# The second product of an MLP in seven quarter products, on groups of 256 tokens

## The chip, the cores and the metric

The kernel runs on one core of one Trainium2 chip. The metric is the device time in microseconds (us), the median of several runs. The profile of the kernel comes from one execution that the hardware profiler recorded.

## The reference, cut to what matters

An attention in blocks, then a layer that mixes by Fourier transforms, then an MLP with two products. There are 4 batches of 768 tokens; a token has 512 numbers (8 heads of 64).

```python
P = sort_net                                   # (4, 8, 8, 8), five rounds of normalizing
k_sorted = einsum('bhij,bhjcd->bhicd', P, k_b) # 8 blocks of 96 tokens, mixed by P
v_sorted = einsum('bhij,bhjcd->bhicd', P, v_b)
attn = softmax(0.125 * q_b @ k_sorted.T)       # inside each block
x = attn @ v_sorted                            # -> (4, 768, 512)
...
u  = x + real(fft(fft(x, axis=1), axis=2))
un = (u - mean(u)) / sqrt(var(u) + 1e-6)
out = u + maximum(un @ w_ch1, 0) @ w_ch2       # 512 -> 2048 -> 512
```

## The kernel before, in words

The work of a batch b falls into three parts.

The **attention**: q and k are loaded as fp16 and turned or mixed on PE (`q_mix`, L785; `k_mix`, L806), v is mixed (`v_mix`, L746) and moved to another layout by DMA (`v_move`, L768). Scores are made on PE (L838), reduced on DVE (L848, L883), raised to the exponential on ACT (L865, L877), and multiplied with the values (L922); DVE normalizes into the tile xr (L928, L929).

The **Fourier part**, which with the norm is called by `post` (L1344): sums and differences of xr on DVE (`fold`, L945, L950), a product over the tokens (`dft_s`, L968 to L990, result W, evacuated by ACT or DVE), sums over W (`fold_d`, L1005), a product over the 512 numbers (`dft_d`, L1030, result PQ by L1043). `residual` (L1073) brings x back to the token order of the output on PE, a copy makes u of it, and `add_res` adds PQ on POOL (L1085, L1086). Then follow the statistics (`stats`, L1100), `root` (L1109, L1113), the normalized un (`normal`, L1123 on ACT or L1126 on DVE), and its transposed form unT (`transpose_u`, L1138 by DMA; in batch 0 on PE, L1147). Tokens come in six tiles of 128, in pairs i = 0, 1, 2 with m = 0, 1.

The **MLP** (`mlp`, L1154) works on two groups of 384 tokens, three tiles, for each batch. For each of 16 chunks of the 2048 hidden numbers, four matmuls with 384 columns make a PSUM bank (L1165), and a relu on ACT or DVE takes it to the fp16 tile hr (L1171). Then, for each of the three tiles of tokens, 16 matmuls with 512 columns add up in a bank (L1183), in four steps of four; one instruction on DVE adds u / 64 and writes the tile outt (L1192), and `store` (L1197) sends it out: by POOL's indirect DMA (L1204), or, for the last two tiles of the last batch, in pieces on SP's and ACT's queues (L1200). All steps of the first and second product write the key "mlp", so that they stay in their written order among themselves.

Nothing of the order between the parts is written out by hand. Each piece of work is a *step* with the engines that can do it and a planned time on each; the planner (`Plan.run`, L396) takes again and again the step that can begin earliest by its own estimate and, among those within 43 ns, the one with the smallest `prio`. The MLP's products have a large prio, so they fill in where others wait; its relus and additions a very small one. The table LEAD (L222) shifts the prio of each kind of step in each batch, and REL (L219) is a time before which a load may not be issued. Loads of q, k, v and of the weights are issued by POOL, one after the other, and before some of them POOL waits, by a small copy (L478), until an earlier one has landed. Up to 69.5 us in the plan, products of the tile junk, which nobody reads, fill the gaps of PE (`fill`, L314; L672).

Buffers are *rings* of tiles: a step that opens a new buffer waits until one in the ring is free. Among them are hr (4 tiles of 4 x 384), u (10), outt (2), unT (2 of 4 x 384), k16 and q16 (3 each), v16 (6) and W (6). The rings k16x and q16x, for batch 0's last pair of heads, lie in a tile of unT. The PSUM has eight banks, one ring.

Of the kernel before, what the change touches and what calls it, by code (L numbers as in the profile page):

```python
# [9 lines left out]
F32 = mybir.dt.float32  # L10
# [5 lines left out]
B = 4  # L16
# [191 lines left out]
class Plan:  # L208
# [4 lines left out]
        psWe=271, psF=430, psR=324, psRh=162, psY=213, ph=640, pc=853, psG=640, psP=60, pcol=60)  # L213
# [8 lines left out]
    LEAD = dict(P=(-69.2, -25.6, 17, -26.9), Q=(0, 14.9, 40, -12.3), We=(2, 19, -0.7, 70.5),  # L222
        Wo=(0, 0, 0, 23.8), a16=(-11.2, 7.7, 69.1, 26.1), a_out=(-16.9, -30.9, -61.8, 4.9),
        add=(-68, 5.4, -30.8, 2.5), amr=(0.9, 0, 0, 0), amt=(-21.4, -19.4, 13.3, 0.1), const=(-1.3, 0, 0, 0),
        exp=(0, -0.4, -24.7, 32.2), fold=(0, -82.7, 0, 0), fold_d=(0, -2.5, -54.6, 0),
        kron=(7.9, 44.5, 27.4, -22.8), kz=(9, 8.3, 19.2, 0), load_k16=(0, 28.3, 2.3, -64.5),
        load_q16=(0, -5, -46.4, -2.3), load_v=(0, 0, 3.1, -3.3), m8=(80.4, 0, 0, 0),
        max=(-23.2, 0, -3.8, -60.5), minus=(50.2, -10.8, -54.2, 2.7), nm=(-36.9, 0, 3.8, 0),
        norm=(-18.9, -61.5, 39.2, 7.1), nse=(-0.9, 0, 0, 0), ot=(14.4, -11.7, -26.5, -37.8),
        outt=(-1.1, 0, 0, -20.8), patch=(77.1, 10.6, 45.9, 21.8), pc=(0, 0, -20.1, 11.7),  # L230
        pca=(-15.9, 0, 0, 0), pcol=(-26, 0, 0, 0), pcs=(-61.4, 0, 0, 0), ph=(-9.7, -14, -8.2, 0),
        psA=(0, -33.9, -24.3, 8.2), psB=(-0.4, 28.7, 8.4, 0), psF=(-46, 22.6, 30, 0), psG=(32.8, 0, 0, 0),
        psK=(6, 17.3, 37.2, 0.7), psM=(2.1, 0, 0, 0), psN=(-31.8, 6.5, 1.2, 0), psP=(-1.1, 0, 0, 0),
        psQ=(59.9, -3.6, 23.4, -2.4), psQK=(0, -29.6, -48.9, -3.2), psR=(12.8, -23.4, 14.8, 14.1),
        psRh=(22.2, 19.3, -2.1, 43.2), psS=(2.6, -28.9, 6.6, 7.3), psT=(14.6, -52.6, 0, 0),
        psV=(-1, 3.9, 20.1, 0), psWe=(38.7, 48, 12, -46.7), psWo=(-4.2, -52.6, -3.4, 8.4),
        psX=(-12.9, 43.1, 13.7, 0), psY=(36, 25.5, 0, 0), psaT=(-20.7, -10.8, 9.5, 1.7),
        ptm=(-45.9, 0, 0, 0), qT=(24.8, 10, 25, 71.4), relu=(0, 0, 0, -22.8), root=(-32.4, 55.6, 42.1, 9),
        row_zero=(-0.4, -51.2, -52.1, -17.7), stats=(10.4, 3.3, 0, 23.2), store=(-20.3, -23.1, -20.8, -3.4),
        turn_e=(0, 0, -27.5, 18.7), u=(-4.7, 56.1, 0, 0.9), un=(58.1, 22, 0, 40.1), unT=(44, 62.4, 0, 15.1),  # L240
        v_move=(0, 21.7, -15.7, 0), v_sum=(0, 0, 28.6, -13.1), vg=(4.3, 0, 0, 0), vo=(-77.8, 6.8, 0, 4.8),
        weights=(9.5, 0, 0, 0), xem=(-0.8, 85.8, -36.2, -9.1), xom=(-50.3, -12.2, 0.6, 0))
# [202 lines left out]
def kernel(  # L445
# [36 lines left out]
    def ring(tag, n, shape, dtype):  # L482
# [938 lines left out]
```

## Time and profile before

| what | value |
|---|---|
| median of 3 runs | 299.06 us (298.74 to 299.49) |
| the profiled execution, first to last instruction (its span) | 300.9 us |
| mean granted clock of PE | 0.979 |
| first product of the MLP (L1165) | 512 matmuls of 384 columns |
| second product (L1183) | 384 matmuls of 512 columns, from 93.6 us on |
| relu (L1171) | 128, 59.9 us on ACT |
| addition of u (L1192) | 24, 16.4 us on DVE |
| last addition begins | 295.68 us |

The profile gives the profiled execution's time as its span alone; it lies 1.8 us above the median of the runs. A line such as `L1165 PE MATMUL bank<-unT,w1sb ... x512 | 89.5, 326 | 1.4 <-DMA ...` names the line of the kernel, the engine, the operation, the tile written and those read, the shape, and the count; then the busy time in us and the mean of one in ns; then how long the engine idled just before such instructions and for what. PE is the matrix engine, PEld its weight loads, DVE the vector engine, ACT the one for functions, POOL and SP the two others. A matmul's duration holds its way through the array, so matmuls that follow each other closely overlap; their true rate is read from a run of them in the chain of waits. The slices cut the span into 40 parts of 7.5 us.

### The profile page before, as it was taken

How to read it: one execution, taken by the hardware profiler on the slowest of the kernel's cores; microseconds unless marked ns; L12 is line 12 of the kernel's file. 1: busy time of each engine (PE TensorE's matmuls, PEld its weight loads, DVE VectorE, ACT ScalarE, POOL GpSimd, SP SyncE). 2: the span in 40 equal slices, each digit the busy share in tenths (PEclk: the TensorE clock that was granted, in tenths of full speed). 3: DMA queues.
4: the chain of work that ended last, by engine and by line, in shares of the span. 5: the costliest groups of instructions: out<-in, count | busy, mean ns of one | idle time of the engine just before them, and what ended most of it. 6: DMA issues, size and time to landing. Idle time of an engine off the chain costs nothing.

```text
span 300.9 us, 6927 instructions
## 1 busy us (share of the span) xinstructions
PE 281.5 (94%) x2616; PEld 163.9 (54%) x2616; DVE 193.0 (64%) x446; ACT 181.8 (60%) x447; POOL 119.4 (40%) x187
## 2 busy tenths in 40 slices
PE   5879999869999999999999989999999999999992
PEld 2454767536775655555645556446655654545541
DVE  6565686999897787565498998988667832001010
ACT  2344797468795687973665589969724741712700
POOL 8445851412032797765646406411013902112010
PEclk9997699999999999999999999999999999999998
DMA  7992995987674657969847833355411123002002
GB/s 103 184 192 70 183 172 94 131 152 130 107 98 73 107 97 138 122 129 180 141 91 137 151 62 77 67 132 123 60 44 37 53 53 105 35 18 89 1 35 72
DMA packets 50848, 30.42 MB, mean 101 GB/s; under 512 B 25962, under 2 KB 48900, under 8 KB 50812
## 3 DMA queue, kind: packets, MB, share of 16 engines
q0 software_dynamic: 19040, 19.40, 38.2%
q1 hardware_dynamic: 31574, 10.28, 16.6%
q8 instruction: 20, 0.33, 0.4%
q10 hardware_dynamic: 200, 0.30, 0.4%
q14 instruction: 14, 0.11, 0.1%
HBM read 28.50 MB, written 6.29 MB: 116 GB/s over the span
## 4 chain that ended last, share of the span: by engine, by line
PE 50%; DMA 27%; DVE 7%; ACT 6%; issue 4%; POOL 3%; SPq 2%; POOLq 0%; DVEq 0%; ACTq 0%
PE bank L1183 19%; PE bank L1165 15%; DMA w2sb<-in_moe_w_ch_dram 8%; DMA eT<-es 4%; DMA w1sb<-in_moe_w_ch_dram 4%; DMA unT<-in_q_dram 3%; DMA v<-in_v_dram 2%; PE bank L838 2%; ACT sm L877 2%; PE bank L968 2%; SPq L768 2%; ACT hr L1171 2%; PE bank L1073 2%; DMA q<-in_q_dram 1%; PE bank L1030 1%
## 5 line engine op out<-in xcount | busy, mean ns | idle before, releaser
L1165 PE MATMUL bank<-unT,w1sb 128*128 128x384 f16 x512 | 89.5, 326 | 1.4 <-DMA unT<-un 0.6
L1183 PE MATMUL bank<-w2sb,hr 128*128 128x512 f16 x384 | 89.7, 379 | 0.4 <-DMA w2sb<-in_moe_w_ch_dram 0.4
L1171 ACT ACTIVATE hr<-bank 128x384 f16<-128x384 f32 x128 | 59.9, 497 | 39.7 <-PE bank L1165 37.8
L1165 PEld LDWEIGHTS <-w1sb 128*128 128x128 f16 x512 | 48.5, 98 | 33.5 <-issue 1.6
L1183 PEld LDWEIGHTS <-hr 128*128 128x128 f16 x384 | 35.9, 98 | 39.5 <-issue 0.7
L1204 POOL DMA_INDIRECT out_dram<-outt,idx_sb x22 | 22.3, 1014 | 87.6 <-DVE outt L1192 52.0
L1192 DVE SCALAR_TENSOR_TENSOR outt<-u,bank 128x512 f32<-128x512 f32 x24 | 16.4, 683 | 49.4 <-PE bank L1183 49.3
L877 ACT ACTIVATE sm<-bank,mns 96x96 f32<-96x96 f32 x128 | 32.3, 352 | 2.5 <-DVE mns L883 2.5
L929 DVE TENSOR_TENSOR xr<-bank,rz 96x512 f16<-96x512 f32 x32 | 22.0, 687 | 1.1
L532 ACT CAST W<-bank 128x384 f16<-128x384 f32 (+1 forms) x33 | 11.3, 380 | 11.4 <-PE bank L968 5.4
L1085 POOL TENSOR_TENSOR u<-u,PQ 128x257 f32<-128x257 f32 x18 | 12.6, 698 | 13.9 <-DVE PQ L1043 9.6
L1100 DVE BATCH_NORM_STATS2 st<-u 128x6 f32<-128x512 f32 x24 | 16.4, 682 | 1.7 <-POOL u L1086 1.7
L848 DVE TENSOR_REDUCE mxs<-bank 96x8 f16<-96x768 f32 x16 | 14.4, 947 | 4.1 <-PE bank L838 3.3
L883 DVE TENSOR_REDUCE mns<-bank 96x8 f32<-96x768 f32 x16 | 15.1, 947 | 3.0 <-PE bank L838 3.0
L554 POOL DMA_DIRECT2D q<-in_q_dram x15 | 10.9, 730 | 10.4 <-PE bank L785 9.8
L534 ACT ACTIVATE kz<-bank 128x768 f16<-128x768 f32 x15 | 11.8, 807 | 4.9 <-PE bank L806 4.8
L865 ACT ACTIVATE sm<-bank 96x768 f32<-96x768 f32 x16 | 12.8, 800 | 3.1 <-PE bank L838 2.2
L928 DVE RECIPROCAL rz<-bank 96x8 f32<-96x8 f32 x32 | 6.4, 199 | 12.7 <-PE bank L922 12.6
L922 PEld LDWEIGHTS <-eT 97*128 97x128 f16 (+1 forms) x256 | 11.2, 101 | 4.4 <-DMA vs<-vo 0.6
L922 PE MATMUL bank<-vs,eT 97*128 97x65 f16 (+1 forms) x256 | 12.4, 196 | 0.8 <-ACT eT L907 0.5
L566 POOL TENSOR_TENSOR vh<-v 128x384 f32<-128x384 f16 x12 | 11.0, 916 | 4.9 <-DMA v<-in_v_dram 4.6
L968 PE MATMUL bank<-cso_sb,xso 120*128 120x384 f16 (+1 forms) x64 | 12.9, 326 | 0.0
(146 smaller groups left out, 433.7 us busy)
## 6 DMA issues: line engine op xcount, KB each, us to landing
vs<-vo SPq DMA_DIRECT2D x48, 65.0 KB
v<-in_v_dram POOLq DMA_DIRECT2D x16, 192.0 KB, 4.9
k<-in_k_dram POOLq DMA_DIRECT2D x15, 192.0 KB, 4.3
q<-in_q_dram POOLq DMA_DIRECT2D x15, 192.0 KB, 4.6
w1sb<-in_moe_w_ch_dram POOLq DMA_DIRECT2D x4, 512.0 KB, 9.4
w2sb<-in_moe_w_ch_dram POOLq DMA_DIRECT2D x4, 512.0 KB, 7.6
eT<-es SPq DMA_TRANSPOSE x32
cdh_sb<-cdh SPq DMA_DIRECT2D x1, 387.0 KB
```

Source lines behind the costliest of these rows:

```text
L848: ("max", b, {"V": 945}, lambda e: nc.vector.tensor_reduce(mxs[n].t.rearrange("p (t j) -> p t j", t=2), pair(pS, BLK), axis=AX.X, op=ALU.max),
L877: nc.scalar.activation(sm.t[:, i], pair(pS, BLK)[:, t, i % 4], AF.Exp, bias=mn.t[:, i:i + 1], scale=-1.0)
L883: ("max", b, {"V": 945}, lambda e: nc.vector.tensor_reduce(mn.t.rearrange("p (t j) -> p t j", t=2), pair(pS, BLK), axis=AX.X, op=ALU.min), ...
L922: nc.tensor.matmul(ps[0:wide(i).stop - BLK * i, i // 4, i % 4], et[0:97, wide(i)], vs[b % 2][:, 4 * y + i % 4, (D + 1) * h:(D + 1) * (h + 1)])
L929: nc.vector.tensor_tensor(xr2[b % 2][0:BLK, 4 * y:4 * y + 4, 128 * hp:128 * hp + 128].rearrange("p j (t d) -> p t j d", t=2), ps[:, :, :, ...
L968: nc.tensor.matmul(ps, x[0:n, j], cso[0:n, j, :], start=(j == 0), stop=(j == 3))
L1100: nc.vector.bn_stats(st.t, us[b, i, m].t)
L1165: nc.tensor.matmul(ps, w1sb[:, mc, 128 * fc:128 * fc + 128], unT[b, gr].t[:, mc, :], start=(mc == 0), stop=(mc == 3))
L1171: nc.scalar.activation(dst, bank(pH, [128, 384]), AF.Relu)
L1183: nc.tensor.matmul(ps, hr[f4].t[:, fc % 4, 128 * t:128 * (t + 1)], w2sb[:, fc, :], start=(fc == 0), stop=(fc == 15))
L1192: step("outt", b, {"V": 687}, lambda e, u=u, pC=pC, o=o: nc.vector.scalar_tensor_tensor(o.t, u.t, RSC, bank(pC, [128, DM]), op0=ALU.mult, ...
L1204: step("store", b, {"G": 1050}, lambda e: nc.gpsimd.indirect_dma_start(out=out.rearrange("b s m -> (b s) m"), out_offset=bass.IndirectOffs ...
```

## The change

The hidden layer times w2 is a product of two matrices that are each cut into two by two quarters. For 256 tokens, h has the quarters a11, a12 (128 tokens; the first and second 1024 hidden numbers) and a21, a22 (the other 128 tokens); w2 has b11, b12, b21, b22. Instead of eight products of quarters the new kernel makes seven (Strassen's scheme in Winograd's form):

```
s1 = a21 + a22   s2 = s1 - a11   s3 = a11 - a21   s4 = a12 - s2
t1 = b12 - b11   t2 = b22 - t1   t3 = b22 - b12   t4 = b21 - t2
pa = a11 b11                 -> out(0,0)     pb = a12 b21  -> out(0,0)
pa = pa + s2 t2              -> out(0,1)     pc = s1 t1
pa = pa + s3 t3              -> out(1,1), and pc to out(1,1)
pa = pa + a22 t4             -> out(1,0)
pc = pc + s4 b22             -> out(0,1)
```

The three groups of a batch are the pairs i of tiles. The sums over h are four steps "hsum" for each group, on DVE (planned 680 ns) or POOL (2450 ns). The sums over w2 are made once, eight steps "w2sum" on POOL alone, and every product waits for all of them; t1, t2 and t4 go to new tiles w2t and t3 takes the place of b12. The quarters of the output are added in place into u, seven instructions with 256 columns on DVE for each group; the tile outt is gone, and u is stored. The key "mlp" is gone: the steps of the MLP are held only by their data. The rings change to make room (hr, hs, u, unT, k16, q16, v16), k16x and q16x lie in two tiles of hr and serve two pairs of heads, m8 lies in a16, and junk is 128 wide and read four times over. The tables REL and LEAD are new throughout; of LEAD only the entries of the MLP are shown.

```diff
-    REL = dict(cdh=19858, cse=8787, cso=15452, idx=79955, load_k1=4655, load_k2=85342, load_k3=87419,
-        load_q1=33423, load_q2=34000, load_q3=131804, load_v1=6381, load_v2=96332, load_v3=14994, rsel=7075,
-        w0=50469, w1=54322, w2=2412, w3=11189, w4=70289, w5=8501, w6=24168, w7=65160)
+    REL = dict(cdh=12758, cse=15250, cso=17105, idx=41973, load_k1=34473, load_k2=84120, load_k3=39047,
+        load_q1=30882, load_q2=49231, load_q3=101588, load_v1=13469, load_v2=56342, load_v3=89242, rsel=0,
+        w0=58699, w1=1283, w2=68579, w3=23248, w4=9287, w5=35406, w6=17841, w7=27269)
...
-    ring("hr", 4, [128, 4, 384], F16)
-    ring("k16", 3, [128, 2, G * D], F16)
-    ring("q16", 3, [128, 2, G * D], F16)
-    ring("v16", 6, [128, 2, G, D], F16)
+    ring("hr", 3, [128, 8, 256], F16)
+    ring("hs", 2, [128, 8, 128], F16)
+    ring("k16", 2, [128, 2, G * D], F16)
+    ring("q16", 2, [128, 2, G * D], F16)
+    ring("v16", 5, [128, 2, G, D], F16)
...
-    ring("u", 10, [128, DM], F32)
+    ring("u", 7, [128, DM], F32)
...
-    ring("unT", 2, [128, 4, 384], F16)
-    ring("outt", 2, [128, DM], F32)
+    ring("unT", 3, [128, 4, 256], F16)
...
+    w2t = [const.tile([128, 8, 256], F16, name=f"w2t{i}") for i in range(3)]
...
-    m8 = const.tile([NB, DM], F16, name="m8")
+    m8 = a16[0:NB]
...
+    def mlp(b, i):
+        h = [Buf("hr") for _ in range(2)]
+        hs = [Buf("hs") for _ in range(2)]
+        u = [us[b, i, m] for m in range(2)]
+        MLP = 1e6 + 1e4 * b + 3e3 * i
+        for y in range(8):
...
+                for x in range(2):
+                    fc = 2 * y + x
+                    for mc in range(4):
+                        nc.tensor.matmul(ps[:, x], w1sb[:, mc, 128 * fc:128 * fc + 128],
+                                         unT[b, i].t[:, mc, :], start=(x == 0 and mc == 0), stop=(mc == 3),
+                                         skip_group_check=True)
...
+                ("ph", b, {"T": 874}, f, [(unT[b, i], j) for j in range(2)] + [("w1", y // 2)], [pH]),
+                ("relu", b, {"A": 590}, g, [pH], [(h[y // 4], y % 4)]), prio=MLP + 50 * y)
...
+        def total(name, out, x, y, op, r, w, k):
+            step("hsum", b, {"V": 680, "G": 2450}, lambda e: plan.engines[e].tensor_tensor(
+                out(), x(), y(), op=op), r=r, w=w, prio=MLP + 400 + k)
+        total("s1", s1, a21, a22, ALU.add, rows[0] + rows[1], [hs[0]], 0)
+        total("s2", s2, s1, a11, ALU.subtract, rows[0] + [hs[0]], [hs[1]], 1)
+        total("s3", a21, a11, a21, ALU.subtract, rows[0] + [hs[0]], [(h[0], "d")], 2)
+
+        pa, pb, pc = Buf("bank"), Buf("bank"), Buf("bank")
+
+        def product(x, w, p, first, r, k, mark=None):
+            def f(e):
+                for fc in range(8):
+                    nc.tensor.matmul(p.t[:, 0:256], x()[:, fc], w[:, fc], start=(first and fc == 0), stop=(fc == 7),
+                                     skip_group_check=True)
+            step("pc", b, {"T": 874}, f, r=r + ([] if first else [p]), w=[p] + ([mark] if mark else []),
+                 prio=MLP + 500 + 100 * k)
+
+        def begin(m, n, p):
+            step("outt", b, {"V": 410}, lambda e: nc.vector.scalar_tensor_tensor(
+                u[m].t[:, HALF[n]], u[m].t[:, HALF[n]], RSC, p.t[:, 0:256], op0=ALU.mult, op1=ALU.add),
+                r=[p, u[m]], w=[(u[m], n)], prio=MLP - 1e8)
+
+        def more(m, n, p):
+            step("outt", b, {"V": 410}, lambda e: nc.vector.tensor_tensor(
+                u[m].t[:, HALF[n]], u[m].t[:, HALF[n]], p.t[:, 0:256], op=ALU.add),
+                r=[p, (u[m], n)], w=[(u[m], n)], prio=MLP - 1e8)
+        wq = [("w2t", y) for y in range(2)]
+        product(a11, w2sb[:, 0:8, HALF[0]], pa, True, rows[0] + wq, 0)
+        begin(0, 0, pa)
+        product(a12, w2sb[:, 8:16, HALF[0]], pb, True, rows[1] + wq, 1, ("p2", b, i))
+        total("s4", a12, a12, s2, ALU.subtract, rows[1] + [hs[1], ("p2", b, i)], [(h[1], "d")], 3)
+        more(0, 0, pb)
+        product(s2, w2t[1], pa, False, [hs[1]] + wq, 2)
+        begin(0, 1, pa)
+        product(s1, w2t[0], pc, True, [hs[0]] + wq, 3)
+        product(a21, w2sb[:, 0:8, HALF[1]], pa, False, [(h[0], "d")] + wq, 4)
+        begin(1, 1, pa)
+        more(1, 1, pc)
+        product(a22, w2t[2], pa, False, rows[1] + wq, 5)
+        begin(1, 0, pa)
+        store(b, i, 1, u[1], MLP - 1e8)
+        product(a12, w2sb[:, 8:16, HALF[1]], pc, False, [(h[1], "d")] + wq, 6)
+        more(0, 1, pc)
+        store(b, i, 0, u[0], MLP - 1e8)
...
+    def w2_sums(y):
+        c = slice(4 * y, 4 * y + 4)
...
+            step("w2sum", 0, {"G": 2450}, lambda e: plan.engines[e].tensor_tensor(
+                out, x, w, op=ALU.subtract), r=r, w=wr, need=70e3 + 1e3 * y)
+        both = [("w2", y), ("w2", y + 2)]
+        go("t1", t1, b12, b11, both, [("t1", y)])
+        go("t3", b12, b22, b12, both + [("t1", y)], [("t3", y)])
+        go("t2", t2, b22, t1, both + [("t1", y)], [("t2", y)])
+        go("t4", t4, b21, t2, both + [("t2", y), ("t3", y)], [("w2t", y)])
...
-        for gr in range(2):
-            mlp(b, gr)
+        for i in range(3):
+            mlp(b, i)
```

More of the change, by code (lines that the diff above doesn't have):

```diff
@@ L518 @@
     for a, tag in enumerate(("k16x", "q16x")):
-        plan.rings[tag] = Ring([plan.rings["unT"].tiles[1][:, 2 * a:2 * a + 2, :]])
+        plan.rings[tag] = Ring([plan.rings["hr"].tiles[y].rearrange("p f t -> p (f t)")[
+            :, 2 * G * D * a:2 * G * D * (a + 1)].rearrange("p (h x) -> p h x", h=2) for y in range(2)])
     def bank(b, shape, dtype=F32):
@@ L1202, in store @@
             return
-        c = 6 * b + q_
+        c = 6 * b + TILE[i, m]
         step("store", b, {"G": 1050}, lambda e: nc.gpsimd.indirect_dma_start(
```

135 lines of the change are left out of this document (59 added, 76 removed).

## The prediction

> **What bounds the kernel now.** I read the page first: the engine shares, then the slices, which say where each engine is full.
>
> ```profile
> PE 281.5 (94%) x2616; PEld 163.9 (54%) x2616; DVE 193.0 (64%) x446; ACT 181.8 (60%) x447; POOL 119.4 (40%) x187
> ...
> PE   5879999869999999999999989999999999999992
> ...
> DVE  6565686999897787565498998988667832001010
> ...
> PEclk9997699999999999999999999999999999999998
> ```
>
> PE is at nine tenths in nearly every slice from the tenth on, at a full granted clock. DVE is the second engine, near full in the middle and almost idle at the end. Since a busy PE is not a PE at its peak, I next took the chain of waits in order of time, where a run of matmuls shows its true rate: its length over its count.
>
> ```profile
> 67.10 7.39 DMA w2sb<-in_moe_w_ch_dram
> ...
> 85.29 8.28 DMA w2sb<-in_moe_w_ch_dram
> ...
> 103.81 0.69 PE bank L1030 x12
> ...
> 224.42 0.34 PE bank L990 x4
> ...
> 243.71 10.36 PE bank L1183 x48
> 254.07 10.40 PE bank L1165 x64
> ...
> 285.23 10.37 PE bank L1183 x48
> 295.68 0.69 DVE outt L1192
> ```
>
> The last 60 us are matmuls of the MLP and nothing else: 64 of the first product (L1165, 384 columns) in 10.40, 162.5 ns each, and 48 of the second (L1183, 512 columns) in 10.36, 215.8 ns each. Then one addition on DVE, and the output's way out. Before about 94 us the chain is loads. The groups give the counts, and the windows where they ran:
>
> ```profile
> L1165 PE MATMUL bank<-unT,w1sb 128*128 128x384 f16 x512 | 89.5, 326 | 1.4 <-DMA unT<-un 0.6
> L1183 PE MATMUL bank<-w2sb,hr 128*128 128x512 f16 x384 | 89.7, 379 | 0.4 <-DMA w2sb<-in_moe_w_ch_dram 0.4
> L1171 ACT ACTIVATE hr<-bank 128x384 f16<-128x384 f32 x128 | 59.9, 497 | 39.7 <-PE bank L1165 37.8
> L1165 PEld LDWEIGHTS <-w1sb 128*128 128x128 f16 x512 | 48.5, 98 | 33.5 <-issue 1.6
> ...
> L1192 DVE SCALAR_TENSOR_TENSOR outt<-u,bank 128x512 f32<-128x512 f32 x24 | 16.4, 683 | 49.4 <-PE bank L1183 49.3
> ```
>
> PE idles 1.8 us in all before these 896 matmuls. So from about 94 us the array is the bound, the MLP fills every hole of the attention, and what shortens the MLP's stream shortens the end, as long as the holes can still be filled.
>
> **The change: the array.** Now 512 x 162.5 ns = 83.2 us and 384 x 215.8 = 82.9 us. After it there are 12 groups of 256 tokens. The first product has 8 x 2 x 4 = 64 matmuls per group, 768 in all; the second has 7 x 8 = 56, 672 in all; all have 256 columns. No row has 256. From the two long runs, 128 columns cost 53.3 ns, 0.417 ns each, and 2.5 ns are fixed; the run of 12 with 129 columns takes 57.5 ns each (3.7 fixed), the run of 4 with 192 or 194 takes 85 (4.6 fixed). That bounds a 256-column matmul between 109.2 and 111.3; I take 110. First product: 768 x 0.110 = 84.5, +1.3 us. Second: 672 x 0.110 = 73.9, -9.0. **Sum -7.7 us** (-8.8 to -5.8 at the ends).
>
> The point to doubt here is the number of weight loads, 896 before and 1440 after. Columns saved are 384 x 512 - 672 x 256 = 24,576, worth 10.2 us; over 544 more pairs the saving is gone if a pair has a fixed cost of 18.8 ns. The rows show 2.5 to 4.6. A load lasts 98 ns, longer than the 57.5 ns at which pairs follow each other at 129 columns, so it does lie under the matmuls.
> The Trainium skill, TensorE: Matmul & The Clock Gate, section Back-to-back issue gap, speaks against the change: it gives streams of load and matmul about 81 ns at 128 columns and 131 ns at 512, so that a pair has a large fixed part. Interpolated, an estimate from that page, 256 columns would take 98 ns and 384 columns 114; the MLP would go from 109 to 141 us, 32 us slower. This trace disagrees at both ends, with 57.5 and 215.8 ns.
>
> **ACT.** 96 relus of 512 columns stand for 128 of 384.
>
> ```profile
> L532 ACT COPY u<-bank x12: 579/586/604, 93.4 to 230.0; 128x512 f32<-128x512 f32 x12
> ...
> L1183 PE MATMUL bank<-w2sb,hr x384: 376/379/390, 93.6 to 295.2; 128*128 128x512 f16 x192
> ```
>
> By the first row (min/median/max in ns, first and last start in us), 96 x 0.586 = 56.3 us for 59.9. Off the chain; 0.
>
> **DVE.** Added are four sums per group of 1024 fp16 elements each, both operands in SBUF, and seven additions of 256 columns from PSUM instead of two of 512. Nearest rows (min/median/max):
>
> ```profile
> L950 DVE TENSOR_TENSOR xse<-xs x24: 276/284/425, 84.0 to 223.8; 96x256 f16<-96x256 f16 x24
> ...
> L945 DVE TENSOR_TENSOR xso<-xr x16: 410/414/661, 42.6 to 224.0; 96x512 f16<-96x512 f16 x16
> ...
> L1005 DVE TENSOR_TENSOR W<-W,W x6: 551/561/562, 94.5 to 226.0; 128x770 f16<-128x770 f16 x6
> ...
> L1043 DVE TENSOR_TENSOR PQ<-bank,ot x24: 393/418/430, 53.6 to 236.0; 128x258 f32<-128x258 f32 x24
> ...
> L1113 DVE SCALAR_TENSOR_TENSOR nm<-mv,rstd x12: 127/154/1572, 63.3 to 242.3; 128x2 f32<-128x2 f32 x12
> ...
> 114.49 1.05 POOL L1204 DMA_INDIRECT out_dram<-outt,idx_sb  x1 [0.44 <-DVE outt L1192]
> ...
> 114.94 1.57 DVE L1113 SCALAR_TENSOR_TENSOR nm<-mv,rstd 128x2 f32<-128x2 f32 x1
> ...
> 115.57 0.92 POOL L566 TENSOR_TENSOR vh<-v 128x384 f32<-128x384 f16 x1
> ```
>
> Going on with the slope from 256 to 512 or that from 512 to 770, a sum takes 674 to 706 ns: 48 x 0.69 = 33.1. The additions: 84 x 0.415 = 34.9, less 16.4. DVE goes from 193 to 245 us, unless the planner gives sums to POOL. The last rows show one more price: a tiny instruction that took 1572 ns once, for 154, from the middle of one POOL instruction to the end of the next. Sums from SBUF may meet the same, above all beside the w2 sums. Where there is room for this:
>
> ```profile
> 20.00:235.00 215.00, 206.36 (x2129) 123.93 (x2124) 166.00 (x364) 151.22 (x379) 93.94 (x151) 0.98 0.63 110
> ...
> 150.00:200.00 50.00, 48.62 (x476) 27.36 (x474) 44.91 (x100) 37.53 (x111) 21.36 (x33) 1.00 0.51 98
> ...
> 235.00:296.00 61.00, 60.59 (x329) 31.70 (x326) 13.95 (x28) 23.39 (x53) 12.40 (x16) 1.00 0.17 52
> ...
> 93.00:235.00 142.00, 58.16 (x240) 21.69 (x239) 1.00 0.56 103
> 235.00:296.00 61.00, 31.57 (x144) 14.09 (x144) 1.00 0.17 52
> ```
>
> The third column of the first three rows is DVE; the last two are L1183 alone. 240 of the 384 second-product matmuls run before 235 us, 7.5 of the 12 new groups: 7.5 x 5.66 = 42.5 us of new DVE work there, less 15 old additions (10.2), so 166 becomes 198 of 215 us, 92%; the densest 50 us now hold 90%. It fits only just, and costs nothing as long as the array has MLP work while the attention waits.
>
> **Waits that are added.** The products of one group share the bank pa: DVE must have read it before the next one adds to it. An outt starts about 0.1 us after its matmul's modelled end, and that end lies 0.16 us after the next matmul could have started (379 - 216 ns); with 0.415 for the reading and about 0.1 to release the next, 0.75 us. Another product lies between the first two reuses; two remain per group, 1.5 us. Queued behind the waiting product on PE is everything else that the order put there. Never hidden this is 12 x 1.5 = 18 us; always hidden, 0. Eleven groups have another group's first product, or attention, to stand in between. The last has nothing behind it: **+1.5 us**. For the other eleven together, and for the attention steps that DVE makes late, I take **+2 us**, near the hidden end, because PE waits so little today.
> At the very end an addition of 256 columns stands in the place of 512: 0.41 for 0.69, **-0.3 us**. The stores behind it stay on the same queues (SP and ACT for the last half group, POOL's indirect ones before), as many as now, and u itself goes out.
>
> **Weights, POOL, rings.** Eight sums over w2, only on POOL, 1024 elements each.
>
> ```profile
> L611 POOL TENSOR_TENSOR kron<-pcs,small_sb x3: 1063/1063/1069, 16.8 to 68.9; 128x512 f16<-128x512 f32 x3
> ...
> L1085 POOL TENSOR_TENSOR u<-u,PQ x18: 626/720/911, 101.8 to 239.3; 128x257 f32<-128x257 f32 x18
> ...
> 20.00:93.00 73.00, 67.56 (x920) 45.84 (x915) 58.68 (x131) 53.21 (x98) 25.73 (x40) 0.93 0.77 123
> ...
> 93.00:104.00 11.00, 5.84 (x24) 2.14 (x23) 1.00 0.60 98
> 93.00:113.00 20.00, 11.87 (x48) 4.19 (x47) 1.00 0.57 95
> ```
>
> By the two POOL rows a sum takes 2.1 to 2.9 us; I take 2.45, so 19.6 in all, four in a chain for each half of w2. No product may start before all eight, where now the first starts at 93.6, as the last block lands (85.29 + 8.28). The release times in the diff move the four w2 blocks forward, to at most 35 us (two were held to 65 and 70), and two w1 blocks back (59 and 69), so I expect w2 to land some 20 us earlier and the sums to be done in time: **0**. If not, see the first rival. The u ring falls from 10 to 7: in the trace the second batch's first u is written at 93.4, when all six of the first batch are still held; afterwards at most one could be. That delays batch 1's residuals; they have slack, as long as other work is there.
> The smaller rings of k, q and v, batch 0's k and q in the hr tiles, m8 inside a16, the smaller junk and the new release times move loads of the first 94 us. What that does I can't cost from a row of its own: in 20 to 93 us (the third row) PE is busy 67.6 of 73 us at a clock of 0.93, so 5.4 us of holes and some of the slow clock are there to win, and as much could be lost; I take **0**, since those holes are waits for loads whose bytes stay the same.
>
> **Sum:** -7.7 + 1.5 + 2.0 - 0.3 + 0 = -4.5 us. The profiled span is 300.9 us, 1.8 above the median of the runs shown (299.06); taken off the span it gives 296.4, off the median **294.5 us**.
>
> **Rivals.** *The w2 sums come late* (the slower side). If w2 still lands at 93.6 with one half unsummed, the products start at 93.6 + 4 x 2.45 = 103.4; with both, at 113.2. There hr holds 1.5 groups of first products, so the array has no MLP work: by the last two rows above, lost are 24 or 48 matmuls' time (5.2 or 10.4 us), with the residuals that wait for u. Each us of delay costs about 0.5, so the 4.5 are gone from a first product at about 103; with 113 and 1.5 us of residuals the time is 294.5 + 11.9 = 306; I take 303. For it: the first row of the chain above, loads to 94 us. Against it: the release times. *DVE and the u ring become the bound:* 198 us at the 90% that the trace shows need 220 of 215, 5 us, and the ring of 7 lets the MLP lag by one group, so little of it is absorbed: 294.5 + 5 = 299.5. For it: the row of 150 to 200. Against it: the 14 of 61 us at the end, and POOL with 94 of 215. *Loads under the matmuls show after all:* 544 x 98 ns - 10.2 = +43, 342 us; the 57.5 ns row is against it. That of the Trainium skill's page is the milder form of this.
>
> **How the numbers follow.** A difference under 0.3% (0.9 us) is not told from none. Forecast 0.60 (all faster). Late sums 0.21 (0.01 same, 0.20 slower). DVE and ring 0.18 (0.02 faster, 0.06 same, 0.10 slower). Loads 0.01. Faster 0.62, same 0.07, slower 0.31. The range goes from 288.5 (all waits hidden at the cheapest matmul with a little over from other places) to 305 (late sums nearly whole); the forecast's own is 288.5 to 298.
>
> **What would show it.** Runs of 256 columns at 109 to 111 ns in the chain; 672 of them in the second product; its first one before 95 us; DVE at 90% or more between 150 and 200 without PE idle before the MLP's lines; gaps of 0.7 us in the last group only. Wrong if PE shows a hole between 80 and 115 us, if products wait for DVE in the middle, or if pairs take more than 115 ns.

## The result, and the profile after

The changed kernel takes 324.01 us (median of 4 runs, 322.34 to 327.60), where the kernel before, measured beside it, takes 298.90 (298.60 to 299.49): 1.085 times as long, 95% interval 1.077 to 1.093. The forecast was 294.5 us in a range up to 305. It was wrong, in sign and by far.

Two things on the numbers that follow. The device time is about 1.8 us more than the profile's span (322.51 and 320.7 for the profiled execution of the changed kernel); over all executions for which both are given it is 1.7 to 2.1 us more, and up to 3.3 in three. And a ratio is taken between undisturbed runs alone while a median is over all runs, so here and there the two differ a little.

The page of the changed kernel, busy time of the engines and the slices (now 8 us each):

```profile
PE 278.9 (87%) x3160; PEld 220.4 (69%) x3160; DVE 254.2 (79%) x528; ACT 181.8 (57%) x424; POOL 182.0 (57%) x212
...
PE   7879998459899898998899969889979899999950
...
DVE  6576879996989788999999999799996937456450
...
PEclk9996999959989999999999989999999999999997
```

PE has holes that it did not have before: one at the eighth and ninth slice (56 to 72 us), and eights through the whole middle. POOL went from 119.4 to 182.0 us, DVE from 193.0 to 254.2. The next view is the chain of waits of the changed kernel, in order of time (start, length, what ended):

```profile
228.20 0.69 DVE hs L1192
229.04 0.69 DVE xr L934
229.72 2.54 DVE hr L1192
232.59 1.66 DVE nm L1118
...
281.00 4.37 PE bank L1203 x40
285.37 3.49 PE bank L1172 x32
...
302.62 0.69 DVE hs L1192
303.64 2.51 DVE hr L1192
306.15 0.66 DVE u L1214 x2
306.82 0.60 DVE hr L1192
307.81 1.05 PE bank L1203 x8
310.12 2.73 DMA out_dram<-u,idx_sb
```

The array does what the forecast said: 40 matmuls of the second product (L1203) in 4.37 us, 109.3 ns each, and 32 of the first (L1172) in 3.49, 109.1 ns. The saving is there. But the chain runs through things that were not on it: sums (L1192) of 2.5 us where others of the same shape take 0.69, and a two-element instruction, nm (L1118), of 1.66. All instructions of these lines on DVE, with the least, median and greatest duration in ns and the first and last start:

```profile
L1192 DVE TENSOR_TENSOR hr<-hr x10: 676/1749/2617, 101.6 to 303.6; 128x1024 f16<-128x1024 f16 x10
L1192 DVE TENSOR_TENSOR hs<-hr,hr x9: 679/692/703, 100.0 to 302.6; 128x1024 f16<-128x1024 f16 x9
...
L1192 POOL TENSOR_TENSOR hs<-hs,hr x7: 2114/2116/2650, 183.2 to 303.5; 128x1024 f16<-128x1024 f16 x7
```

```profile
L1118 DVE SCALAR_TENSOR_TENSOR nm<-mv,rstd x12: 128/157/4610, 59.1 to 283.1; 128x2 f32<-128x2 f32 x12
```

```profile
L1214 DVE TENSOR_TENSOR u<-u,bank x36: 389/420/422, 105.2 to 311.3; 128x256 f32<-128x256 f32 x36
```

A sum takes 0.68 us on DVE and 2.12 on POOL, but the third sum of a group takes 1.75 at the median, and nm 4.61 at its worst. The third row is the contrast: an addition with an operand in PSUM never takes more than 0.422. What goes on during the long ones is seen in the timeline of the changed kernel, here its hole at 60 us (start, length, engine, line, tile written and those read):

```profile
58.88 2.13 POOL L1255 TENSOR_TENSOR w2t<-w2sb 128x1024 f16<-128x1024 f16 x1
...
59.12 1.92 DVE L1118 SCALAR_TENSOR_TENSOR nm<-mv,rstd 128x2 f32<-128x2 f32 x1
...
61.69 2.13 POOL L1255 TENSOR_TENSOR w2sb<-w2sb 128x1024 f16<-128x1024 f16 x1
...
62.09 4.61 DVE L1118 SCALAR_TENSOR_TENSOR nm<-mv,rstd 128x2 f32<-128x2 f32 x1
...
63.76 0.77 POOL L1271 DMA_DIRECT2D w1sb<-in_moe_w_ch_dram  x1
64.55 2.13 POOL L1255 TENSOR_TENSOR w2t<-w2sb,w2t 128x1024 f16<-128x1024 f16 x1
...
67.62 1.01 PE L1078 MATMUL bank<-xr,rsel_sb 99*128 99x512 f16 x2 [4.77 <-DVE mxs L853]
```

The first nm begins 0.24 us after POOL's sum over w2 began, and ends at 61.04, as that sum ends (61.01). The second begins 0.40 us into the next sum and ends at 66.70, as the sum after that ends (66.68). In between POOL issues a DMA, and DVE does not get in. Everything of DVE stands behind: PE waits 4.77 us for a reduction (L853). The windows of 60 to 80 us, first of the changed kernel, then of the kernel before (PE, PEld, DVE, ACT, POOL busy; then the granted clock):

```profile
60.00:80.00 20.00, 13.47 (x171) 10.16 (x170) 17.19 (x26) 12.01 (x20) 9.73 (x8) 0.74 0.59 95
```

```profile
60.00:80.00 20.00, 17.18 (x243) 11.41 (x242) 18.81 (x45) 15.06 (x31) 3.32 (x5) 1.00 0.81 139
```

DVE is called busy for 17.19 of 20 us and finishes 26 instructions, where it finished 45; PE loses 3.7 us, and the mean granted clock of the window is 0.74. A busy share does not tell work from standing still.

In this order, the first product of the second kind comes at 100.1 us (before: 93.6). By then the sums over w2 are long done; POOL's last two are

```profile
88.69 4.33 POOL L1255 TENSOR_TENSOR w2t<-w2sb,w2t 128x1024 f16<-128x1024 f16 x2
```

and end at 93.02. At the other end, the timeline of the changed kernel around its last products:

```profile
303.49 2.11 POOL L1192 TENSOR_TENSOR hs<-hs,hr 128x1024 f16<-128x1024 f16 x1 [6.08 <-DVE hs L1192]
303.56 2.59 DVE L1192 TENSOR_TENSOR hr<-hr 128x1024 f16<-128x1024 f16 x1
...
306.56 11.16 SPq L1240 DMA_DIRECT2D out_dram<-u  x5
...
310.12 0.99 POOL L1244 DMA_INDIRECT out_dram<-u,idx_sb  x1 [4.52 <-DVE u L1214]
...
311.29 0.42 DVE L1214 TENSOR_TENSOR u<-u,bank 128x256 f32<-128x256 f32 x1 [0.45 <-PE bank L1203]
313.62 0.96 POOL L1244 DMA_INDIRECT out_dram<-u,idx_sb  x1 [2.51 <-DMA out_dram<-u,idx_sb]
```

The last group has the same pair once more, a sum on POOL and one on DVE begun 0.07 us apart. And the last addition ends at 311.71, 9.0 us ahead of the span's end; in the kernel before it was 4.5 (295.68 + 0.69, and 300.9). The second indirect store waits until the first has landed, and SP's pieces of the last half group are under way until 317.72.

### The profile page after: what moved, and what is told of

It is laid out like the page before. It is cut to its first block, busy times and chain, and to the rows that moved or that the text cites. A ratio compares the mean times of both kernels' runs of the same rounds, so it can differ in the third digit from the quotient of the medians.

```text
span 320.7 us, 8062 instructions
## 1 busy us (share of the span) xinstructions
PE 278.9 (87%) x3160; PEld 220.4 (69%) x3160; DVE 254.2 (79%) x528; ACT 181.8 (57%) x424; POOL 182.0 (57%) x212
## 4 chain that ended last, share of the span: by engine, by line
PE 44%; DVE 27%; ACT 10%; DMA 7%; POOL 6%; issue 4%; POOLq 0%; SPq 0%; DVEq 0%; ACTq 0%
PE bank L1172 14%; PE bank L1203 12%; ACT sm L882 4%; DMA hr<-in_k_dram 3%; DVE hr L1192 3%; DMA eT<-es 3%; PE bank L843 3%; DVE nm L1118 2%; ACT hr L1179 2%; PE bank L973 2%; DVE xr L934 2%; DVE vo L762 2%; PE bank L865 2%; DVE u L1209 2%; DVE W L1010 2%
## 5 line engine op out<-in xcount | busy, mean ns | idle before, releaser
L1172 PE MATMUL bank<-unT,w1sb 128*128 128x256 f16 x768 | 94.9, 276 | 0.8 <-DVE W L539 0.7
L1172 PEld LDWEIGHTS <-w1sb 128*128 128x128 f16 x768 | 73.8, 99 | 12.4 <-issue 1.2
L1179 ACT ACTIVATE hr<-bank 128x512 f16<-128x512 f32 x96 | 56.4, 598 | 37.3 <-PE bank L1172 37.0
L1203 PEld LDWEIGHTS <-hr 128*128 128x128 f16 x480 | 46.3, 98 | 13.4 <-issue 6.9
L1244 POOL DMA_INDIRECT out_dram<-u,idx_sb x22 | 25.6, 1164 | 50.1 <-DVE u L1209 20.5
L1203 PE MATMUL bank<-w2sb,hr 128*128 128x256 f16 x384 | 49.0, 276 | 5.1 <-DVE u L1209 5.1
L1209 DVE SCALAR_TENSOR_TENSOR u<-u,bank 128x256 f32<-128x256 f32 x48 | 19.7, 410 | 6.9 <-PE bank L1203 6.9
L1203 PE MATMUL bank<-w2t,hs 128*128 128x256 f16 x192 | 25.0, 279 | 0.2 <-POOL hs L1192 0.2
L1192 POOL TENSOR_TENSOR hs<-hs,hr 128x1024 f16<-128x1024 f16 x7 | 15.4, 2195 | 16.9 <-DVE hs L1192 15.6
L1203 PEld LDWEIGHTS <-hs 128*128 128x128 f16 x192 | 18.8, 100 | 3.2 <-POOL hs L1192 0.5
L1105 DVE BATCH_NORM_STATS2 st<-u 128x6 f32<-128x512 f32 x24 | 16.4, 682 | 3.5 <-POOL u L1091 3.4
L1192 DVE TENSOR_TENSOR hs<-hr,hr 128x1024 f16<-128x1024 f16 x9 | 6.2, 692 | 15.5 <-ACT hr L1179 15.4
L853 DVE TENSOR_REDUCE mxs<-bank 96x8 f16<-96x768 f32 x16 | 14.9, 948 | 2.4 <-PE bank L843 2.2
L1192 DVE TENSOR_TENSOR hr<-hr 128x1024 f16<-128x1024 f16 x10 | 16.5, 1651 | 0.0
```

The costliest lines, as they stand in the source:

```text
L853: ("max", b, {"V": 945}, lambda e: nc.vector.tensor_reduce(mxs[n].t.rearrange("p (t j) -> p t j", t=2), pair(pS, BLK), axis=AX.X, op=ALU.max),
L1105: nc.vector.bn_stats(st.t, us[b, i, m].t)
L1172: nc.tensor.matmul(ps[:, x], w1sb[:, mc, 128 * fc:128 * fc + 128], unT[b, i].t[:, mc, :], start=(x == 0 and mc == 0), stop=(mc == 3), skip ...
L1179: nc.scalar.activation(dst, bank(pH, [128, 2, 256]), AF.Relu)
L1192: step("hsum", b, {"V": 680, "G": 2450}, lambda e: plan.engines[e].tensor_tensor(out(), x(), y(), op=op), r=r, w=w, prio=MLP + 400 + k)
L1203: nc.tensor.matmul(p.t[:, 0:256], x()[:, fc], w[:, fc], start=(first and fc == 0), stop=(fc == 7), skip_group_check=True)
```

## The theories

**The lock.** While POOL runs an instruction on SBUF, a DVE instruction that works within SBUF (two operands there, or a plain copy) stands still until POOL ends. POOL's sums are 2.1 us long, so each may cost DVE up to that, and it is a price of where the sums run.

**The load.** DVE simply has too much: 61 us more busy time in the trace.

**The order.** The new release times, rings and LEAD table lose time in the loads and in the middle, whoever makes the sums.

## Experiments that let the planner choose a new order

`all_dve` allows the 48 group sums and the 8 sums over w2 on DVE only; `hsum_dve` and `w2sum_dve` do one of the two:

```diff
-            step("hsum", b, {"V": 680, "G": 2450}, ...
+            step("hsum", b, {"V": 680}, ...
-            step("w2sum", 0, {"G": 2450}, ...
+            step("w2sum", 0, {"V": 690}, ...
```

> The changed kernel with all sums, those over h and those over w2, on DVE alone; the planner lays out its order anew. Lock theory (while POOL executes a sum of 1024 elements, DVE's instructions whose operands all lie in SBUF stand still, and everything behind them on DVE too): the stretched instructions go back to their usual length (the tiny nm to 0.15 us at the median and under 1.6 at the most, the sums to 0.69), the hole between 58 and 80 us closes, the time falls by 10 to 20 us, to 303 to 312. Load theory (DVE has too much to do, whoever holds the port): 17 more sums of 0.69 us and 8 over w2 make 17 us more for DVE, the time rises by 3 to 10 us. Ring theory (the smaller rings and the new order are what costs): within 3 us of the changed kernel.

> The changed kernel with only the sums over h bound to DVE; the eight over w2 stay on POOL. Lock theory: the hole between 58 and 80 us stays, the stretching after 100 us goes; gain 5 to 10 us, to 312 to 317. Load theory: slower by 2 to 8 us. Ring theory: within 3 us.

> The changed kernel with only the eight sums over w2 moved from POOL to DVE. Lock theory: the hole between 58 and 80 us closes (there nm stands for 1.9 and 4.6 us), gain 6 to 10 us, to 312 to 316, the stretching after 100 us stays. Load and ring theory: within 3 us of the changed kernel, since 5.5 us of DVE at 60 to 90 us are little.

The fourth tells the planner that a group sum on DVE, like the other steps of that list, has to wait until POOL's instruction is over, where it believed in 0.45 us at the most:

```diff
-    PORT, PORT_WAIT = ("fold", "fold_d", "minus", "nm", "un", "xem"), 450.0
+    PORT, PORT_WAIT = ("fold", "fold_d", "minus", "nm", "un", "xem", "hsum"), 5000.0
```

> The changed kernel, but the planner believes that a DVE instruction on SBUF operands (the sums over h now among them) waits until POOL's instruction is over, where it believed 0.45 us at the most. Sums may still go to either engine. Lock theory: with the right price the planner keeps the two apart; fewer sums on POOL beside DVE's, gain 4 to 12 us. Load and ring theory: within 3 us.

Measured: `all_dve` 323.68 us, ratio 1.088 [1.082, 1.094]; `hsum_dve` 326.33, 1.091 [1.082, 1.099]; `w2sum_dve` 337.05, 1.130 [1.123, 1.138]; `port` 340.30, 1.148 [1.141, 1.156]. None is faster than the changed kernel, and two are slower by a good ten us. All four miss what the lock foretold for the time, and read plainly this would be against it. But every one of them also has another order of all its work: the planner, given other engines or times, decides everything anew, and the tables REL and LEAD were made for the old decisions. In the trace of `all_dve` nm never takes more than 0.280 us, so the stretching is gone as foretold, and yet the time is the same: the new order must lose as much elsewhere, and where stays open. As a test of what the sums cost, the four are inconclusive, and the change to the method is their result. From here on the planner decides as in the changed kernel, with the same times and the same order on every engine, and only what a step *executes* is altered.

## Experiments in the kept order: which engine makes the sums

`hsum_moved` is the changed kernel with the 17 group sums of POOL executed by DVE, at the place that they have in the order:

```diff
-        s.fn(e)
+        s.fn("V" if s.name == "hsum" else e)
```

> The changed kernel with its order kept on every engine to the instruction; only the 17 sums over h that ran on POOL stand on DVE, at the place that they had in the plan. Lock theory (POOL's long sums hold DVE): DVE's stretched instructions between 100 and 310 us go back to their length, 5 to 15 us faster than the changed kernel, 307 to 317. Load theory: 12 us more for DVE, slower by 2 to 8 us. Ring theory: within 3 us.

`no_hsum` leaves the 48 group sums out (the products read a11 and a21 in the place of s2 and s1, so they are not the reference's):

```diff
-        s.fn(e)
+        if s.name != "hsum":
+            s.fn(e)
```

> The order kept, but all 48 sums over h left out: the products read unsummed quarters, so part of the computation is missing. Lock theory and load theory both: 12 to 20 us faster than the changed kernel, what the sums cost wherever they run; the hole at 58 to 80 us stays. Ring theory: 0 to 4 us faster.

`no_w2sum` leaves the 8 sums over w2 out in the same way (the products read quarters of w2 itself), and `no_sums_same` leaves out both kinds.

> The order kept, but the eight sums over w2 left out: the products read w2's own quarters, so part of the computation is missing. Lock theory: nm at 59 and 62 us goes back from 1.9 and 4.6 us to 0.15, PE's hole there and the slow clock after it go, 6 to 10 us faster. Load theory and ring theory: 0 to 3 us faster.

> The order kept, both kinds of sums left out (part of the computation is missing); the array's work, the additions from PSUM, the rings and the tables are the changed kernel's. Lock and load theory: the whole loss is the sums, so 288 to 296 us. Ring theory: the loss stays, 312 or more.

Measured: `hsum_moved` 313.38 us, 1.048 [1.035, 1.061]; `no_hsum` 307.19, 1.027 [1.019, 1.035]; `no_w2sum` 315.30, 1.057 [1.049, 1.065]; `no_sums_same` 298.73, 0.996 [0.990, 1.002].

So giving DVE 17 *more* sums made the kernel 10.6 us *faster*. That rules out the load as main cause: it foretold the other sign. In the rows of `hsum_moved` the third sums are short at the median, and of nm only the two beside the w2 sums still stand, the longer of them as long as before:

```profile
L1192 DVE TENSOR_TENSOR hr<-hr x12: 677/683/1395, 102.0 to 294.4; 128x1024 f16<-128x1024 f16 x12
```

```profile
L1118 DVE SCALAR_TENSOR_TENSOR nm<-mv,rstd x12: 128/152/4602, 59.2 to 273.4; 128x2 f32<-128x2 f32 x12
```

The page of `hsum_moved` says how much of DVE's busy time had been standing still:

```profile
PE 276.8 (89%) x3160; PEld 219.1 (71%) x3160; DVE 244.1 (79%) x545; ACT 181.6 (59%) x424; POOL 146.3 (47%) x195
```

DVE is busy for 10.1 us less than the 254.2 of the changed kernel, with 17 sums more. At 0.6 us for each of these (the distance of sums that follow each other), about 20 us had been waiting, an estimate. A rival is that a sum on POOL is simply longer, 2.12 us for 0.68, and that the products wait for it. The chain of waits of the changed kernel speaks against this: of the 17 it holds one whole sum, 2.39 us at 264.27, so that the rival is worth some 2 us of the 10.6.

Leaving all group sums out gives 6.2 us beyond that; so much the 48 sums cost as work on DVE. And `no_sums_same` is 25.3 us faster than the changed kernel, just what the two parts give together (16.8 and 8.7). It has all the new rings, release times and LEAD, so the order as such cannot have made the kernel slower than before. But it only equals the kernel before, where the array alone should save 7.7, and it missed the 288 to 296 us expected of it.

Is it really nm that makes the w2 sums dear? `nm_act` leaves the sums on POOL and makes nm by three small instructions on ACT, at the same place:

```diff
-        step("nm", b, {"V": 160}, lambda e: nc.vector.scalar_tensor_tensor(...
+            for m in range(2):
+                nc.scalar.activation(nms[b, i].t[:, m:m + 1], mv[b, i].t[:, m, 0:1], AF.Copy,
+                                     scale=rstd[b, i].t[:, m:m + 1])
+            nc.scalar.mul(nms[b, i].t, nms[b, i].t, -1.0)
+        step("nm", b, {"V": 160}, minus_mean, r=...
```

> The changed kernel, its order kept, with one tiny instruction moved: nm (minus the mean over the deviation, 12 times in all) is made by three small instructions on ACT where DVE made it with operands in SBUF. Lock theory in its sharp form (POOL's two sums over w2 cost time because nm stands on DVE for 1.9 and 4.6 us and un, the transposes and the first products wait for it): most of the 8.7 us that the w2 sums cost come back, 316 to 320. If the w2 sums cost time by filling POOL's queue ahead of loads: within 2 us of the changed kernel. ACT's 12 x 0.6 us more are covered.

Measured: 317.07 us, 1.064 [1.054, 1.075], 6.9 us less, by taking twelve instructions of 0.15 us off DVE (in the changed kernel five of the twelve stood for over 1 us, two of them beside the sums over w2). In its timeline POOL's sums are as long as ever, and DVE goes on beside them:

```profile
62.74 2.13 POOL L1258 TENSOR_TENSOR w2t<-w2sb 128x1024 f16<-128x1024 f16 x1
```

```profile
62.98 0.74 DVE L1048 TENSOR_TENSOR PQ<-bank,ot 128x258 f32<-128x258 f32 x2
63.63 0.55 DVE L762 SCALAR_TENSOR_TENSOR vo<-a,bank 128x384 f16<-128x384 f16 x1
64.09 0.95 DVE L853 TENSOR_REDUCE mxs<-bank 96x8 f16<-96x768 f32 x1
```

All three read PSUM, and none is longer than elsewhere. Nor is a statistic of u (L1105), which reads a single operand from SBUF: it takes 0.69 us at 65.74, beside the next sum. It is not POOL being busy that hurts here; it is one DVE instruction with both operands in SBUF, at the wrong moment.

Do the two places of the lock add? `moved_nm` is `hsum_moved` and `nm_act` in one; `all_moved` has the w2 sums executed by DVE too:

```diff
-        s.fn(e)
+        s.fn("V" if s.name in ("hsum", "w2sum") else e)
```

> The 17 group sums go from POOL to DVE in the frozen order, and nm is made by three small instructions on ACT; the w2 sums stay on POOL. If the two places of the lock are separate, the gains add: 324.0 - 10.6 - 7 = 306 to 308. If the gains are one and the same (the same holes of PE filled twice over), it stays at 313.

> All sums of the changed kernel, the 17 group sums and the 8 sums over w2 that POOL made, are made by DVE at the same places of the frozen order. If POOL's long sums shut out DVE and the two stalls add, the time is that of the kernel with moved group sums (313.4) less the 8.7 that leaving out the w2 sums gave, plus at most 8 x 0.69 = 5.5 for the new work on DVE: 305 to 310, and no instruction nm of over 1 us while w2 is summed. If the load of DVE were the cause, 25 more sums on it would make it slower than the 313.4.

Measured: `moved_nm` 306.45 us, 1.029 [1.020, 1.037]; `all_moved` 304.91, 1.016 [1.006, 1.026], a hair under what was expected. They add: `moved_nm` is 17.6 us below the changed kernel, and 10.6 and 6.9 make 17.5. In `moved_nm` the group sums no longer hold nm, so its 6.9 us below `hsum_moved` are those of nm beside the sums over w2 alone. In `all_moved` the row of nm, which had 4610, is

```profile
L1118 DVE SCALAR_TENSOR_TENSOR nm<-mv,rstd x12: 127/151/161, 62.2 to 267.6; 128x2 f32<-128x2 f32 x12
```

and the first group sum starts at 94.0 us instead of 100.0. It has the lowest time of the versions that make all the sums, 19.1 us better than the changed kernel, and still 1.6% slower than the one before.

## The same sums in the kernel before

`before_sums` is the kernel before with the price alone and none of the gain: POOL makes 8 subtractions of 1024 elements that nobody needs, two behind each load of a w2 block, in the old order. `before_again` is the kernel before, unchanged, for a second trace.

```diff
...
+            for _ in range(2):
+                two = junk[:, None, :].broadcast_to([128, 2, DM])
+                nc.gpsimd.tensor_tensor(scratch, two, two, op=ALU.subtract)
```

> The kernel before, with its order, and eight subtractions of 1024 fp16 elements on POOL, two behind the issue of each w2 block (at about 53, 68, 76 and 86 us); they read a constant tile, and what they write is not read. PE, ACT, DVE and the data of the rest are untouched. Lock theory: DVE's instructions on SBUF operands that fall beside them (nm near 70, the folds near 86) stand for 2 us, and the time rises by 2 to 8 us. If POOL's sums cost only by POOL's own time, which waits for loads there anyway: within 1 us of the kernel before.

> The kernel before as it is, for a profile from the same chips. Every theory: ratio 1 within 0.5%; its profiled span about 1.8 us under its own device time, as for the changed kernels.

Measured: `before_sums` 304.34 us, 1.024 [1.016, 1.031]; `before_again` 297.69, 0.998 [0.993, 1.003]. Eight instructions of 1.9 us, whose result nobody reads, on an engine that is idle six tenths of the time, cost 5 us or more. In the timeline of `before_sums`, then the row of the same line in `before_again`:

```profile
71.22 0.80 POOL L1221 DMA_DIRECT2D w2sb<-in_moe_w_ch_dram  x1
71.58 2.65 DVE L705 COPY xse<-xso 24x1024 f16<-24x1024 f16 x1
72.03 3.95 POOL L1235 TENSOR_TENSOR outt<-junk 128x1024 f16<-128x1024 f16 x2
```

```profile
L705 DVE COPY xse<-xso x3: 423/423/426, 69.4 to 173.6; 24x1024 f16<-24x1024 f16 x3
```

A copy within SBUF goes from 0.42 to 2.65 us. A rival is that POOL's loads come later. Those behind the first pair of subtractions do (k at 54.2 us for 50.0), but the later blocks of w2 do not (71.22 and 80.76 us for 71.64 and 81.27), and it is between 70 and 90 us that PE is busy for 16.9 us where it was busy for 19.9. So the lock needs neither Strassen's scheme nor the new order.

## The end

What of the 7.7 us did `no_sums_same` lose? Its last addition ends at 288.29 and its span at 296.4, 8.1 us for the old 4.5. The first attempt, on the changed kernel, sent the last two direct half groups out by POOL's indirect DMA as well (`exit_indirect`: the condition for the direct pieces is replaced by False); the second, `no_sums_exit`, is `no_sums_same` with the last two indirect stores left out, a half of each of the last two groups:

```diff
+        if b == B - 1 and i > 0:
+            return
         c = 6 * b + TILE[i, m]
```

> The changed kernel, all other work in its order, with the last batch's two half groups that went out in pieces on SP's and ACT's queues sent by POOL's indirect DMA like the rest. In the changed kernel the direct and the indirect stores of the last two groups alternate and each waits for the other kind to land, so 9.0 us lie between the last addition and the end, 4.5 before. If that alternation is the cause: 2 to 4 us faster. If the way out is bound by the DMAs themselves: within 1 us.

> The kernel without any sums (298.7), with the last two indirect stores of the last batch (one half of each of its last two groups) left out, so that no store of the end stands behind another one's landing. If the missing rest of the array's saving lies in the stores that follow each other at the end, the end after the last addition goes from about 8 us back to the 4.6 of the kernel before, and the time to 295 +- 1. If the stores only share the same way out of bytes and nothing waits, it stays within 1 us of 298.7.

Measured: `exit_indirect` 325.27 us, 1.094 [1.086, 1.102], no gain; `no_sums_exit` 295.11, 0.983 [0.977, 0.989]. In the timeline of `exit_indirect`, POOL's last three:

```profile
312.03 0.96 POOL L1244 DMA_INDIRECT out_dram<-u,idx_sb  x1 [2.51 <-DVE u L1209]
315.55 0.97 POOL L1244 DMA_INDIRECT out_dram<-u,idx_sb  x1 [2.56 <-DMA out_dram<-u,idx_sb]
319.04 0.97 POOL L1244 DMA_INDIRECT out_dram<-u,idx_sb  x1 [2.52 <-DMA out_dram<-u,idx_sb]
```

They follow 3.5 us apart, the last two waiting for the landing of the one before: the miss is that I had taken the kind of store for the cause, where it is the number of stores that are late. In `no_sums_exit` no indirect store stands behind the last direct ones, and the last addition ends 4.0 us ahead of the span's end:

```profile
286.35 0.42 DVE L1215 TENSOR_TENSOR u<-u,bank 128x256 f32<-128x256 f32 x1 [0.45 <-PE bank L1204]
```

(286.77 and 290.8). So the exit has a price: the ratio goes down by 1.3 points, 3.8 us. Two stores fewer are also fewer bytes; that the waiting counts, and not the bytes, is read from the waits in the timelines alone.

## Why the prediction was wrong, point by point

Taken as ratios, so that chips drop out, and in us of 298.7, the account from the kernel before to the changed one is:

| step | ratio | us |
|---|---|---|
| no sums, no late indirect stores (`no_sums_exit`) | 0.983 | -5.1 |
| the stores at the end (`no_sums_same`) | 0.996 | +3.8 |
| all sums as work on DVE (`all_moved`) | 1.016 | +6.1 |
| the sums over w2 on POOL (`hsum_moved`) | 1.048 | +9.5 |
| 17 group sums on POOL (the changed kernel) | 1.085 | +11.1 |

Each ratio has an interval of 0.6 to 1.3 points to either side, so a single step is sure to some 2.5 to 5 us.

**The array, -7.7 us: right.** 109.1 to 109.3 ns for 256 columns, at the lower bound of 109.2 to 111.3. The weight loads lie under the matmuls; with 1440 pairs, the rival that they would show is refuted, and so are the 32 us more that the forecast worked out from the Trainium skill, TensorE: Matmul & The Clock Gate, section Back-to-back issue gap.

**Added waits, +3.5 us, and rings and loads, 0: in agreement as a sum, not tested one by one.** Without sums and late stores the scheme gives -5.1 us where array, waits and the last addition were to give -4.5. But PE's idle time just before the second product is 1.0 us in `no_sums_same` and 3.1 in `all_moved`, and the mean granted clock of `no_sums_same` is 0.961 to 0.977 where the kernel before beside it has 0.975 to 1.00. So other losses are in this sum, and that it comes out so near is in part luck.

**ACT, 0: right.** 56.4 us for 96 relus, forecast 56.3.

**DVE, 0: mis-sized.** The sums at 0.68 us are as long as forecast, but "It fits only just, and costs nothing as long as the array has MLP work while the attention waits" was wrong by 6.1 us, for the 48 and the eight together. A window at 92% on the average has stretches near 100%: in `all_moved` DVE is busy for 19.3 to 19.7 of every 20 us from 120 to 180. That this is how the 6.1 us arise is argued, not shown: PE is busy for 57.0 of these 60 us, and for 56.4 in `no_sums_same`, which has no sums at all. The second rival had this mechanism at 5 us.

**The sums on POOL, 0: the step that failed.** Of the weight sums the forecast asked only whether they would be *done in time*. They were, at 93.0 us. For the group sums it took POOL, with 94 of 215 us to do, as room that takes load off DVE. What a sum on POOL does to DVE in the meantime stood at nothing; it costs 9.5 us for the weight sums and 11.1 for the group sums. The row that shows it stood in the prediction, nm at 1572 ns for 154 between two POOL instructions, with the sentence "Sums from SBUF may meet the same, above all beside the w2 sums"; it was noted and not priced. By that row, POOL's 25 sums of 2.1 us are 53 us in which DVE can be held, and with DVE at 92% hardly any of it falls into its free time; only what DVE does from PSUM goes on. Half of it, 26 us, a mere guess, would have been nearer than 0 (measured: 20.6).

The Trainium skill, SBUF — State Buffer, section Who interferes with whom, says that the pair of ports which DVE shares with GpSimd (POOL) is an exclusive lock, held for the whole instruction by the one that came first, and that it binds DVE in a two-port mode, or with two SBUF inputs against a GpSimd instruction that reads SBUF. The rows above of POOL's sums agree with it, also in what escapes (operands from PSUM). One goes further: the 4.61 us of nm are more than one POOL instruction, and a DMA issue lies among them.

**The end, -0.3 us: wrong by some 4 us.** That the stores behind it stay on the same queues, as many as now, is true and does not matter. A group is now 256 tokens whose four quarters are completed in its last products: the last two halves of the output are ready 0.9 us apart (310.84 and 311.71), where the last two tiles were 3.5 us apart (292.92 and 296.37). So the stores of the end come closer together, and they wait for each other.

**The rivals.** "Late sums" had the first product at 103.4 us and a time of 303, and it came at 100.1; but not by that mechanism, since the sums were done 7 us earlier. What came late is DVE's and PE's other work, held by the lock: with all sums on DVE the first product is at 94.8. That 303 lies on the right side is luck. None of the rivals had the lock.

**What the first trace of before overstated.** Its span of 300.9 is, with the 1.8 us, a device time of 302.7, 3.6 above the 299.06; `before_again` has a span of 294.9. The last 52 us ahead of the last addition are the same in both, so what it held too much lies earlier, such as 1.5 of the 1.8 us of idle before L1165 and L1183 (0.3 in `before_again`). The forecast took its time from the median, so this does not bear on the miss.

What stays open: where in the middle the 6.1 us of DVE's work come onto the path was not taken apart further; the u ring of 7, the other part of the second rival, was not tested alone; and whether a freshly searched order with all sums on DVE beats the kernel before was not tried. By the table it would need to win back the 6.1 us or the 3.8 at the end.

## What to carry to other kernels

An idle POOL is not a free one: price each instruction that it gets on SBUF as a stall of DVE, up to its whole length, wherever DVE works from SBUF (two operands, or a copy) at the same time, and look in the trace for tiny DVE instructions whose greatest duration is many times the median. In a kernel whose order was planned, hold the order fixed when you test one cause; otherwise the experiment measures the planner. And when the unit of work at the end gets smaller, count the stores that become ready after the last product, not the bytes.

## What was not expected of the hardware

- A DVE instruction that waits for POOL can be passed over: nm was held for 4.61 us, over the rest of one POOL sum, a DMA issue and the whole of the next sum. A DMA issue holds it too: in the first trace of the kernel before, nm, at its usual 0.15 us, would have been over at 115.09, during an indirect issue (114.49 to 115.54) and ahead of POOL's next instruction (115.57); it ended at 116.51, with that instruction.
- It seems to go both ways. In the changed kernel, an indirect store's issue took 3.27 us (the others 0.96 to 1.46) while DVE made three sums within SBUF one after the other. Where the group sums are left out, no such issue takes more than 1.07:

```profile
118.12 3.27 POOL L1244 DMA_INDIRECT out_dram<-u,idx_sb  x1 [0.54 <-DVE es L900]
...
118.60 0.68 DVE L1192 TENSOR_TENSOR hs<-hs,hr 128x1024 f16<-128x1024 f16 x1
119.20 0.68 DVE L1192 TENSOR_TENSOR hr<-hr 128x1024 f16<-128x1024 f16 x1
119.80 0.68 DVE L1192 TENSOR_TENSOR hr<-hr,hs 128x1024 f16<-128x1024 f16 x1
```

- The hole in PE may cost twice. In the changed kernel PE is busy for 1.2 of the 6 us from 62 to 68, and from 68 to 74 it is busy throughout at a granted clock of 0.53; in the kernel before the clock is 1.00 there. That the hole causes it is not shown: in `no_sums_same`, with PE busy for 5.99 us from 62 to 68, the clock of that stretch is 0.72.
